# Half of the q and k transposes by the DMA crossbar, a reordered opening, sixteen matmuls moved to an earlier stage, and states scaled as soon as they are made

## The chip, the cores and the metric

The kernel runs on one core of one Trainium2 chip. The metric is device microseconds (us) per execution. Each timed kernel is run several times, in the same rounds as the kernel before on the same chip; I quote medians. "PE" is TensorE, "ACT" ScalarE, "DVE" VectorE, "POOL" GpSimd, "SP" SyncE.

## The reference, cut to what matters

Decayed linear attention (4 batches, 8 heads, 768 positions, head size 64), followed by a two-layer MLP (512 to 2048 to 512) with an ELU between the layers.

```python
# attention, per block; S is a state per head that decays and is carried along
intra = (q k^T * Dmask) v
inter = (q * lam^(pos+1)) S
out   = intra + inter
S     = lam^block * S + (k * rev_pow)^T v
# MLP on x = [3072, 512]
h = x @ w_in ;  g = where(h > 0, h, exp(min(h, 0)) - 1) ;  y = g @ w_out
```

## The kernel before

The kernel works in chunks of 128 positions of one batch: 24 chunks, numbered so that four in a row (one of each batch) make one MLP tile of 512 tokens. There are six tiles. While the MLP of a tile runs, the attention of the next tile is slipped in between its steps, two chunks per "visit". A visit has three places in the step list: transposes of q and k, then scores and mask, then output and state.

```python
def att_T(g, n, which, tag="S"):           # PE transposes q or k into PSUM
    ...
    nc.tensor.transpose(pt[:, j, i, hp, :], in_=nat[:, 2*hp : 2*hp+2, :], identity=ident16[:])
def att_Te(g, n, which, eng):              # ACT evicts them to SBUF, as qT and kT
    ...
    nc.scalar.copy(out=dst[:], in_=pt[:, j])

def att_tmp(g, eng="p"):                   # POOL: tmp = old state * lam^128
    ...
    e.tensor_tensor(out=tmp[r], in0=old[r, :, :, r], in1=up_p[r]..., op=ALU.mult)
def att_st(g):                             # DVE: new state = tmp + U (U is in PSUM)
    ...
    nc.vector.tensor_tensor(out=new[r, :, :, r], in0=tmps[g][r], in1=pu[r], op=ALU.add)

def mm1(t, n):  # 4 matmuls into psH, then ACT: e = exp(psH), r = relu(psH)
def elu(...):   # DVE: g = min(e - 1, r)
def mm2(t, i, n):  # one matmul of chunk i into psM; after n = 15 the eviction and the store

def visit(g, s0, s1, s2):
    at(s0, att_T / att_Te for q and k); at(s0, att_kd, g, 2)      # kd = k * ks, on DVE
    at(s1, att_S, g); at(s1, att_S, g+1); at(s1, att_mask, ...)   # P = psS * mask, on DVE
    at(s2, att_tmp, g)                                            # scaling, just ahead of its use
    at(s2, att_O, g, 2); at(s2, att_U, g); at(s2, att_X, g, 2); at(s2, att_st, g)

# steps: (name, mm1 of that step, [mm2 of that step])
('A', n): mm1 of tile 0, n = 0..15; from n = 10 mm2 of its chunks 0 and 1
('B', n): no mm1: mm2 of chunks 0 and 1 of tile 0 (B6 to B15), and attention of tile 1
(1, n):   mm1 of tile 1, and two mm2 of chunks 2 and 3 of tile 0
(2, n) to (5, n): mm1 of the tile, four mm2 of the tile before
```

In the opening, q, k and v of chunk 0 come as float32 over the hardware queues (SP, ACT) and are cast on DVE and ACT. All else comes over POOL's queue, which casts to fp16 on the way.

## Time and profile before

The kernel takes 229.4 us. Milestones, read from the starts of the exps (ACT, `e<-psH`; there are 16 per tile) in the trace:

| | first exp | 16th exp (end of A) | 17th (tile 1) | 33rd (tile 2) | 81st (tile 5) | span |
|---|---|---|---|---|---|---|
| before | 21.8 | 43.9 | 55.5 | 83.7 | 183.1 | 227.5 |

The window view gives the busy time of each engine between such milestones: after each window its length, then busy time (instructions) by engine, granted clock, DMA share, and GB/s.

```profile
core 0: us, PE busy (x) PEld busy (x) DVE busy (x) ACT busy (x) POOL busy (x), PEclk, DMA share, GB/s
0.00:21.80 21.80, 11.75 (x110) 6.41 (x111) 11.98 (x24) 9.60 (x21) 19.55 (x28) 1.00 1.69 152
21.80:43.90 22.10, 19.67 (x139) 8.85 (x138) 16.11 (x24) 16.58 (x31) 16.94 (x16) 0.92 1.79 180
43.90:83.70 39.80, 37.62 (x423) 21.07 (x422) 33.68 (x41) 24.59 (x42) 29.34 (x27) 1.00 2.46 167
83.70:183.10 99.40, 99.40 (x824) 50.85 (x822) 72.41 (x86) 65.28 (x114) 9.40 (x7) 1.00 0.34 43
```

In the fourth window PE is busy for the whole 99.40 us. In the three before it, several engines share the chain. A busy PE in this view is not a full PE, because matmuls overlap. So I also use a stricter count. PE's work is what its matmuls need back to back, as the trace shows them when nothing holds them (four of 512 columns in 0.86 us, sixteen transposes of 128 columns in 0.89 us, half of that for the paired ones on half the array); what is left between the starts of matmuls is idle.

| stretch of the kernel before | length | PE work | PE idle |
|---|---|---|---|
| 16th to 17th exp (the B steps) | 11.6 | 9.3 | 2.3 |
| 17th to 33rd exp (tile 1) | 28.2 | 26.2 | 2.0 |
| 33rd exp to 209 us (tiles 2 to 5) | 125.3 | 122.6 | 2.7 |

The page of the kernel before, in 40 slices (tenths): PE, the granted clock, and the DMA engines.

```profile
PE   0488969989998999999999999999999999999993
...
PEclk9999988999999999999999999999999999999999
DMA  4999999999999999210110110110110011001212
```

The granted clock is 0.5 for one stretch of 3.4 us, from 32.9 us, in the first pass. The DMA engines are full until about 90 us; nearly all of that is loading.

One line of waits (who waited for whom: us in total, times, longest):

```profile
DVE st L346 <- POOL tmp L328: 1.8, 3, 1.1
```

### The profile page before, as it was taken

To read this page: it belongs to the slowest core of one execution; us is meant where nothing else is said; L and a number is where in the kernel's file an instruction comes from. 1 tells how busy PE (TensorE), PEld (TensorE's weight loads), DVE (VectorE), ACT (ScalarE), POOL (GpSimd) and SP (SyncE) were. 2 spreads that over 40 slices of the span, in tenths; PEclk is the share of its full clock that TensorE was granted. 3 is DMA by queue.
4 is the path that set the end of the run, shared out by engine and by line. 5 is a ranking of instruction groups with operands and counts; after the bars stand their busy time and mean duration, and the time that the engine had idled before them with its cause. 6 is when DMAs were issued, how large, how long until landed. Compare 5 with 4: busy or idle time off the path is not lost.

```text
span 227.5 us, 4119 instructions
## 1 busy us (share of the span) xinstructions
PE 209.0 (92%) x1673; PEld 105.4 (46%) x1673; DVE 148.3 (65%) x193; ACT 135.9 (60%) x244; POOL 75.2 (33%) x75
## 2 busy tenths in 40 slices
PE   0488969989998999999999999999999999999993
PEld 0353425546454554554554554555455444444441
DVE  2549885798876999997887667647537544534110
ACT  4562686733859587576576576576486466676110
POOL 8899947838677893130220000000000000000000
PEclk9999988999999999999999999999999999999999
DMA  4999999999999999210110110110110011001212
GB/s 97 171 163 186 189 162 173 196 163 156 197 157 153 174 156 158 68 46 3 46 48 3 46 49 0 46 49 1 46 49 31 15 49 46 37 20 39 92 50 89
DMA packets 83971, 20.59 MB, mean 91 GB/s; under 512 B 76144, under 2 KB 81008, under 8 KB 83952
## 3 DMA queue, kind: packets, MB, share of 16 engines
q0 software_dynamic: 77088, 13.24, 84.3%
q1 hardware_dynamic: 5680, 6.69, 8.8%
q10 hardware_dynamic: 1184, 0.39, 0.7%
q8 instruction: 13, 0.21, 0.4%
q14 instruction: 6, 0.05, 0.1%
HBM read 27.27 MB, written 6.29 MB: 148 GB/s over the span
## 4 chain that ended last, share of the span: by engine, by line
PE 73%; DVE 10%; ACT 9%; issue 3%; DMA 2%; POOL 1%; SPq 0%; DVEq 0%; ACTq 0%
PE psM L387 33%; PE psH L359 29%; DVE P L256 5%; PE psT L210 4%; ACT e L364 3%; DMA q_first<-in_q_dram 2%; DVE g L379 2%; PE psO L269 2%; PE psS L244 2%; ACT r L368 2%; DVE xt L293 2%; PE psO L277 1%; ACT qT L221 1%; ACT kT L221 1%; POOL tmp L328 1%
## 5 line engine op out<-in xcount | busy, mean ns | idle before, releaser
L359 PE MATMUL psH<-xt,wi 128*128 128x512 f16 x384 | 98.8, 382 | 2.4 <-ACT r L368 2.3
L379 DVE SCALAR_TENSOR_TENSOR g<-e,r 128x512 f16<-128x512 f32 x92 | 68.6, 758 | 46.0 <-ACT r L368 45.4
L387 PE MATMUL psM<-wo,g 128*128 128x512 f16 x384 | 98.1, 381 | 0.0
L364 ACT ACTIVATE e<-psH 128x512 f32<-128x512 f32 x96 | 58.0, 605 | 57.9 <-PE psH L359 55.6
L359 PEld LDWEIGHTS <-wi 128*128 128x128 f16 x384 | 37.6, 98 | 48.7 <-issue 4.9
L368 ACT ACTIVATE r<-psH 128x512 f16<-128x512 f32 x92 | 55.4, 602 | 0.0
L387 PEld LDWEIGHTS <-g 128*128 128x128 f16 x384 | 35.6, 98 | 40.1 <-issue 0.6
L256 DVE TENSOR_TENSOR P<-psS,mask 128x1024 f16<-128x1024 f32 (+1 forms) x28 | 28.7, 1065 | 4.1 <-PE psS L244 3.8
L328 POOL TENSOR_TENSOR tmp<-st,up_p 64x512 f32<-64x512 f16 x16 | 20.2, 1261 | 22.6 <-DVE st L346 21.6
L293 DVE TENSOR_TENSOR xt<-psO,qs 128x1024 f16<-128x1024 f32 (+2 forms) x15 | 14.9, 1004 | 6.3 <-PE psO L277 5.4
L221 ACT COPY qT<-psT 128x1024 f16<-128x1024 f16 (+1 forms) x14 | 12.6, 896 | 7.1 <-PE psT L210 7.1
L78 POOL DMA_DIRECT2D kn<-in_k_dram x13 | 14.3, 1103 | 5.3 <-issue 4.7
L78 POOL DMA_DIRECT2D vn<-in_v_dram x13 | 14.5, 1114 | 4.5 <-issue 2.9
L78 POOL DMA_DIRECT2D qn<-in_q_dram x13 | 14.7, 1132 | 3.7 <-issue 1.8
L407 ACT COPY osb<-psM 128x512 f32<-128x512 f32 x12 | 7.1, 592 | 14.6 <-PE psM L387 14.6
L210 PE MATMUL psT<-ident,qn 128*128 128x128 f16 x96 | 8.4, 231 | 7.7 <-DVE qn L162 7.3
L269 PE MATMUL psO<-P,vn 128*64 128x128 f16 x192 | 12.6, 227 | 1.3 <-DVE P L256 0.8
L269 PEld LDWEIGHTS <-vn 128*64 128x64 f16 x192 | 10.1, 111 | 7.1 <-issue 6.2
L221 ACT COPY kT<-psT 128x1024 f16<-128x1024 f16 (+1 forms) x14 | 12.8, 916 | 0.0
L231 DVE TENSOR_TENSOR kd<-kn,ks 128x1024 f16<-128x1024 f16 x10 | 12.3, 1229 | 0.0
L210 PEld LDWEIGHTS <-qn 128*128 128x128 f16 x96 | 6.9, 103 | 11.7 <-DVE qn L162 7.3
L346 DVE TENSOR_TENSOR st<-tmp,psU 64x512 f16<-64x512 f32 x16 | 10.9, 681 | 2.0 <-POOL tmp L328 1.8
(43 smaller groups left out, 97.8 us busy)
## 6 DMA issues: line engine op xcount, KB each, us to landing
out_dram<-osb SPq DMA_DIRECT2D x23, 256.0 KB, 2.0
qn<-in_q_dram POOLq DMA_DIRECT2D x10, 256.0 KB, 12.9
kn<-in_k_dram POOLq DMA_DIRECT2D x10, 256.0 KB, 13.0
vn<-in_v_dram POOLq DMA_DIRECT2D x10, 256.0 KB, 13.2
wo<-in_moe_w_out_dram POOLq DMA_DIRECT2D x4, 512.0 KB, 14.0
wi<-in_moe_w_in_dram POOLq DMA_DIRECT2D x2, 512.0 KB, 6.8
wi<-in_moe_w_in_dram POOLq DMA_DIRECT2D x3, 256.0 KB, 6.8
qn<-in_q_dram POOLq DMA_DIRECT2D x3, 128.0 KB, 7.6
```

Of the source, the lines that this page charges most:

```text
L78: nc.gpsimd.dma_start(out=dst, in_=src[b : b + n, :, rows].rearrange("b h p d -> p (b h) d"))
L210: nc.tensor.transpose(pt[:, j, i, hp, :], in_=nat[:, 2 * hp : 2 * hp + 2, :], identity=ident16[:],)
L221: nc.scalar.copy(out=dst[:], in_=pt[:, j])
L256: nc.vector.tensor_tensor(out=P[:, :, c], in0=s[:, :, c], in1=mask[:, :, c], op=ALU.mult)
L269: nc.tensor.matmul(po[r, i, hp, :], lhsT=v_of(g + i, 2 * hp + hh), rhs=P[:, hh, hp, :], start=True, stop=(c == 0), skip_group_check=True,)
L293: nc.vector.tensor_tensor(out=xt[t][:, c, i * L : (i + n) * L].rearrange("p h (n l) -> p n h l", n=n), in0=po[:, :, c], in1=qs[:, c].unsqu ...
L328: e.tensor_tensor(out=tmp[r], in0=old[r, :, :, r], in1=up_p[r].unsqueeze(1).unsqueeze(3).broadcast_to([64, 2, HP, 64]), op=ALU.mult,)
L359: nc.tensor.matmul(pH[:], lhsT=wi[:, kk, j * 128 : (j + 1) * 128], rhs=xt[t][:, kk, :], start=(kk == 0), stop=(kk == HP - 1),)
L364: nc.scalar.activation(e[:], pH[:], AF.Exp)
L368: nc.scalar.activation(r[:], pH[:], AF.Relu)
L379: nc.vector.scalar_tensor_tensor(out=gt[t][:, n, :], in0=e[:], scalar=-1.0, in1=r[:], op0=ALU.add, op1=ALU.min)
L387: nc.tensor.matmul(pm[:], lhsT=gt[t][:, n, i * L : (i + 1) * L], rhs=wo_t[wo_at[n][0]][:, wo_at[n][1], :], start=(n == 0), stop=(n == NF - 1),
```

## The change

Its intent has three parts.

1. **Crossbar.** q and k of chunks 12 to 23 are transposed by DMA, from the loaded SBUF tiles to SBUF, instead of by PE with an eviction on ACT. The Trainium skill, "DMA: Bandwidth & Descriptors", section "DMA Transpose (X-bar)", says that the plain DMA transpose can be issued by the hardware queues only and that it takes 2-byte types; the kernel keeps to both (SP, fp16).
2. **Opening.** Chunk 0 comes over POOL's casting queue, first in line. Transposes of q and k are separate, with filler matmuls (`warm`) between. The states are cleared by DVE; `kd` of the first four chunks goes to POOL, and their state copies to ACT and to later steps (A8, A10). The first three hidden blocks of tile 0 are computed early, on the 384 columns that are there before chunk 3 (the "prefill").
3. **Middle.** The 16 `mm2` of chunk 2 of tile 0 move from tile 1 into the B steps (the "fill"). A state is scaled right after it is made ("early scaling"), not just ahead of its use.

Smaller edits came along: from tile 1 on the third place of a visit lies one step later, the visit in B lies one step earlier, hidden block 1 of tile 0 takes the ordinary path of exp and relu, and `tmp` has three buffers where it had two.

```diff
-    LOADS = [(1, 1, 'q'), (1, 1, 'k'), (1, 1, 'v'), (2, 1, 'q'), ...
+    LOADS = [(0, 1, 'q'), (0, 1, 'k'), (0, 1, 'v'), (1, 1, 'q'), ..., ('kd', 0), ('wi', 6), ('kd', 2), ...
+    def att_xT(g):
+        for j, ts in enumerate((qn, kn)):
+            dst = asb.tile([128, 2 * HP, 128], FP16, tag=f"{w}T", ...)
+            nc.sync.dma_start_transpose(out=dst[:], in_=heads(ts, g, 2).rearrange("p h d -> p (h d)"))
+    XT = {12: (1, 10), 14: (2, 2), 16: (2, 10), 18: (3, 2), 20: (3, 10), 22: (4, 2)}
     def visit(g, s0, s1, s2):
+        if g in XT:
+            at(XT[g], att_xT, g)
+        else: (transposes on PE as before)
-        at(s2, att_tmp, g)
         at(s2, att_O, g, 2)
         ...
         at(s2, att_st, g)
+        at(s2, att_tmp, g + B)
... (cut: opening, order of transposes, scores and warm-ups; prefill with mm1_mm(0, n, 0, 3 * L); places of the visits) ...
-(('B', 0), None, []), ...            ((1, 0), (1, 0), [(0, 2, 0), (0, 2, 1)]), ...
+(('B', 0), None, [(0, 2, 0)]), ...   ((1, 0), (1, 0), [(0, 3, 0)]), ...
```

## The prediction

> **What bounds the kernel now.** The stage view (busy time by windows) and the chain of waits show three regimes.
>
> 1. Opening, 0 to 20.8 us. The first full matmul of the MLP starts at 20.79 us. The chain begins with the load of q of chunk 0 (issued 1.17, landed 6.77 us) and then crawls through casts, ScalarE copies and VectorE masks. The loads of chunks 1 to 3, issued by POOL from 1.36 us, land 7.6 us after issue; they advance by about 0.87 us per 128 KB.
> 2. 20.8 to about 83 us: PE alternates with ScalarE and VectorE. In tile 0's first pass ScalarE needs 1.2 us per step (exp 605 ns, relu 602 ns) for 0.86 us of matmul; the granted clock even falls to 0.5 at 34 to 36 us. From about 45 to 54 us (the steps without new hidden activations) I count 6.8 us of PE work in 9.2 us, and the next tile, 54.3 to 83.2 us, holds 25.6 us of PE work in 28.9 us.
> 3. 83 us to the end: PE is never idle in the window view; the chain is matmul after matmul (four in 0.86 us). ScalarE (65%) and VectorE (50 to 80%) have room there.
>
> **What the change does.**
> - Transposes of chunks 12 to 23 leave PE: six groups of 16, each 0.89 us in the chain, all in regime 3. That is 5.3 us, all on the critical path. Twelve ScalarE evictions (1.03 us each) go too, off the path. In their place come twelve 256 KB crossbar DMAs on the SP queue, issued 8 steps (about 14 us) before use. The Trainium skill, "Advanced Engine Details and Errata", section X-Bar Transpose (TRN2), says they run as fast as ordinary DMAs. No trace here shows one yet. At the 12 to 16 us that loads need under the present traffic even the first would be just in time; later ones meet an idle DMA. I expect no PE wait from them.
> - Opening: chunk 0 goes first on the casting queue without the three 256 KB loads beside it and without two DVE casts (0.43 and 0.79 us) and one ScalarE cast. I estimate q of chunk 0 at about 5 us, v of chunk 3 at 15 to 16 us (16.0 now), and the first exp near 18 to 18.5 us instead of 21.85: gain about 3.5 us. Three hidden blocks are computed on three quarters of the columns beforehand. After that ScalarE still binds (about 21.8 us for the first pass, against 20 now), so little more comes there.
> - Refill: 16 output matmuls (3.5 us) move from the next tile into the steps without hidden activations, filling the holes there; that tile then is bound by ScalarE and VectorE at about 24 to 25 us. Early state scaling removes POOL waits (1.8 us before the state adds; 2.1 us of POOL scaling lies in the chain near 65 us). Together about 2 us.
>
> Sum: 5.3 + 3.5 + 2 = 10.8 us.
>
> **Prediction:** 218.8 us, range 214.5 to 224. Faster by over 2%: 0.91; within 2%: 0.08; slower by over 2%: 0.01.
>
> **What would show it.** PE transposes 192 down to 96; each half stage from 83 us on 16.7 down to about 15.8 us; first exp near 18 us; the stretch from the first step without hidden activations to the second tile's end 2 us shorter; SP transposes landing within 10 us; no PE wait on a transposed tile.
>
> **What would make it wrong.** Crossbar transposes far slower than ordinary loads, or slowing the POOL loads, so that scores wait for qT or kT; the first POOL load still landing 7 us after issue, which would hold the opening; ScalarE in the second tile costing more than the filling gains; output stores held up behind a waiting transpose on SP.

## More of the kernel before

POOL runs its instructions in order: DMA issues, `tmp`, and (before the change) the clearing of the states.

Groups of instructions of the kernel before that the change touches (busy, mean ns of one, idle before and its releaser):

```profile
L379 DVE SCALAR_TENSOR_TENSOR g<-e,r 128x512 f16<-128x512 f32 x92 | 68.6, 758 | 46.0 <-ACT r L368 45.4
...
L328 POOL TENSOR_TENSOR tmp<-st,up_p 64x512 f32<-64x512 f16 x16 | 20.2, 1261 | 22.6 <-DVE st L346 21.6
...
L231 DVE TENSOR_TENSOR kd<-kn,ks 128x1024 f16<-128x1024 f16 x10 | 12.3, 1229 | 0.0
...
L210 PE MATMUL psT<-ident,qn 128*128 128x128 f16 x96 | 8.4, 231 | 7.7 <-DVE qn L162 7.3 <-DVE xt L293 0.3
L210 PE MATMUL psT<-ident,kn 128*128 128x128 f16 x96 | 8.4, 230 | 0.1
```

## The result, and the profile after

The changed kernel takes 220.41 us (220.04 to 222.15, four runs), the kernel before 229.43. The ratio is 0.9617, with a 95% interval of 0.9558 to 0.9675. A ratio here is the mean time of one kernel's runs over that of the other's of the same rounds, so it is not quite the ratio of the medians. Timed a second time (experiment 9), it was 220.21 us, ratio 0.9605.

| | first exp | 16th | 17th | 33rd | 81st | span |
|---|---|---|---|---|---|---|
| before | 21.8 | 43.9 | 55.5 | 83.7 | 183.1 | 227.5 |
| after | 20.1 | 39.7 | 54.6 | 79.4 | 173.8 | 218.6 |
| gained so far | 1.7 | 4.2 | 0.9 | 4.3 | 9.3 | 8.9 |

The last row reads the result: 4.2 us are gained by the end of the first pass (A), 3.3 of them are lost again in the B steps, and come back in tile 1. From the 33rd to the 81st exp 5.0 us are gained, evenly.

The window view of the changed kernel:

```profile
0.00:20.10 20.10, 15.02 (x130) 7.51 (x131) 12.25 (x25) 9.54 (x21) 19.09 (x26) 1.00 1.63 127
20.10:39.70 19.60, 17.00 (x133) 7.98 (x131) 16.61 (x18) 17.72 (x33) 18.18 (x17) 1.00 1.80 183
39.70:79.40 39.70, 37.87 (x412) 20.69 (x413) 36.59 (x42) 24.67 (x42) 29.77 (x26) 1.00 2.19 172
79.40:173.80 94.40, 94.40 (x737) 45.92 (x736) 70.82 (x87) 55.00 (x103) 12.14 (x10) 1.00 0.79 84
```

The third window, B and tile 1 together, is as long as before (39.70 against 39.80 us), and DVE is now busy for 36.59 us of it instead of 33.68. In the fourth window PE is still always busy, with 87 fewer matmul records and 5.0 us less.

The slices of the changed kernel: in this profile the clock does not dip. (One of its four timed runs, the one of 222.15 us, has a mean clock of 0.992; more on this before the experiments.)

```profile
PE   5979789899998999999999999999999999999992
...
PEclk9999999999999999999999999999999999999999
DMA  6999999999999999999143052061011011110221
```

DMA issues of the changed kernel (count, size, median us from issue to landing); the two lines of the transposes.

```profile
qT<-qn SPq DMA_TRANSPOSE x6, 5.2
kT<-kn SPq DMA_TRANSPOSE x6, 5.2
```

The median hides two groups: six transposes that ran beside the loads landed 6.6 to 11.9 us after issue, the six later ones after 3.2 to 3.8 us. No line of the waits names a DMA of qT or kT.

The groups and the wait that answer to those shown before:

```profile
L398 DVE SCALAR_TENSOR_TENSOR g<-e,r 128x512 f16<-128x512 f32 x93 | 71.3, 780 | 37.5 <-ACT r L387 37.3
...
L336 POOL TENSOR_TENSOR tmp<-st,up_p 64x512 f32<-64x512 f16 x16 | 21.6, 1347 | 21.2 <-DVE st L355 20.3
...
L239 DVE TENSOR_TENSOR kd<-kn,ks 128x1024 f16<-128x1024 f16 x8 | 11.5, 1443 | 0.0
...
L206 PE MATMUL psT<-ident,kn 128*128 128x128 f16 x32 | 2.5, 219 | 0.7 <-DMA kn<-in_k_dram 0.7
L206 PE MATMUL psT<-ident,qn 128*128 128x128 f16 x32 | 2.4, 219 | 0.0
```

With 32 more of the opening, in tiles of their own (`psTq`, `psTk`), 96 transposes are left on PE.

The wait of the state add on POOL's scaling is gone from the list, but `kd` has become slower (1443 ns against 1229) and so has `g` (780 against 758). The timeline shows why. Each line has start, duration, engine, instruction, count. First the kernel before, where the scaling runs from 38.34 to 40.97 us, mostly in a pause of DVE of 2.12 us:

```profile
36.35 0.69 DVE L379 SCALAR_TENSOR_TENSOR g<-e,r 128x512 f16<-128x512 f32 x1 [1.37 <-ACT r L368]
...
36.96 1.22 DVE L231 TENSOR_TENSOR kd<-kn,ks 128x1024 f16<-128x1024 f16 x1
...
38.28 0.69 DVE L379 SCALAR_TENSOR_TENSOR g<-e,r 128x512 f16<-128x512 f32 x1
38.34 2.63 POOL L328 TENSOR_TENSOR tmp<-st,up_p 64x512 f32<-64x512 f16 x2
...
41.09 0.69 DVE L379 SCALAR_TENSOR_TENSOR g<-e,r 128x512 f16<-128x512 f32 x1 [2.12 <-ACT r L368]
```

Then the changed kernel, where four scalings run from 32.30 to 38.24 us:

```profile
29.35 0.68 DVE L398 SCALAR_TENSOR_TENSOR g<-e,r 128x512 f16<-128x512 f32 x1
...
31.97 1.94 DVE L398 SCALAR_TENSOR_TENSOR g<-e,r 128x512 f16<-128x512 f32 x1 [0.29 <-ACT r L387]
...
32.30 5.94 POOL L336 TENSOR_TENSOR tmp<-st,up_p 64x512 f32<-64x512 f16 x4
...
33.84 2.06 DVE L239 TENSOR_TENSOR kd<-kn,ks 128x1024 f16<-128x1024 f16 x1
...
35.82 2.97 DVE L398 SCALAR_TENSOR_TENSOR g<-e,r 128x512 f16<-128x512 f32 x2
...
38.71 2.34 DVE L264 TENSOR_TENSOR P<-psS,mask 128x1024 f16<-128x1024 f32 x2
```

A `g` needs 0.68 us alone and 1.94 us here; a `kd` 1.22 alone and 2.06 here. The Trainium skill, "SBUF — State Buffer", section "Who interferes with whom", says that a DVE instruction with two SBUF inputs contends with a GpSimd instruction that reads SBUF, and that the second of the two blocks until the first is done. The trace agrees: `g` (e and r) and `kd` (kn and ks) have two SBUF inputs and are slowed; `st`, whose second input is in PSUM, took 692 ns beside the scaling and 677 alone. Over the whole changed kernel 13 of 93 `g` ran beside the scaling, at 1344 ns against 689 for the others. Up to the 33rd exp this costs DVE about 7.3 us more than the same instructions alone; in the kernel before it is 2.5 us.

### The profile page after: what moved, and what is told of

Same layout as the page of the kernel before. It is cut to its first block, busy times and chain, and to the rows that moved or that the text cites. A ratio compares the mean times of both kernels' runs of the same rounds, so it can differ in the third digit from the quotient of the medians.

```text
span 218.6 us, 3968 instructions
## 1 busy us (share of the span) xinstructions
PE 204.8 (94%) x1593; PEld 100.3 (46%) x1593; DVE 150.3 (69%) x190; ACT 126.8 (58%) x234; POOL 79.2 (36%) x76
## 4 chain that ended last, share of the span: by engine, by line
PE 71%; DVE 13%; POOL 5%; ACT 5%; issue 2%; DMA 2%; DVEq 0%; POOLq 0%; ACTq 0%
PE psM L406 34%; PE psH L372 30%; DVE g L398 5%; DVE P L264 3%; PE psO L277 2%; DMA vn<-in_v_dram 2%; ACT e L383 2%; ACT r L387 2%; DVE kd L239 2%; POOL qn L72 2%; POOL kn L72 2%; PE psO L285 2%; PE psS L252 2%; POOL vn L72 1%; DVE st L355 1%
## 5 line engine op out<-in xcount | busy, mean ns | idle before, releaser
L372 PE MATMUL psH<-xt,wi 128*128 128x512 f16 (+2 forms) x396 | 98.0, 372 | 2.8 <-DVE g L396 1.1
L398 DVE SCALAR_TENSOR_TENSOR g<-e,r 128x512 f16<-128x512 f32 x93 | 71.3, 780 | 37.5 <-ACT r L387 37.3
L336 POOL TENSOR_TENSOR tmp<-st,up_p 64x512 f32<-64x512 f16 x16 | 21.6, 1347 | 21.2 <-DVE st L355 20.3
L72 POOL DMA_DIRECT2D vn<-in_v_dram x14 | 15.4, 1102 | 4.2 <-issue 4.2
L426 ACT COPY osb<-psM 128x512 f32<-128x512 f32 x12 | 7.0, 591 | 16.1 <-PE psM L406 16.1
L72 POOL DMA_DIRECT2D qn<-in_q_dram x14 | 15.7, 1124 | 1.4 <-issue 1.4
L72 POOL DMA_DIRECT2D kn<-in_k_dram x14 | 15.3, 1091 | 1.9 <-issue 1.9
L424 DVE COPY osb<-psM 128x512 f32<-128x512 f32 x11 | 7.6, 689 | 5.9 <-PE psM L406 5.8
L239 DVE TENSOR_TENSOR kd<-kn,ks 128x1024 f16<-128x1024 f16 x8 | 11.5, 1443 | 0.0
L355 DVE TENSOR_TENSOR st<-tmp,psU 64x512 f16<-64x512 f32 x16 | 10.9, 680 | 0.2
L285 PE MATMUL psO<-qT,st 128*64 128x128 f16 x160 | 10.3, 219 | 0.0
L285 PEld LDWEIGHTS <-st 128*64 128x64 f16 x160 | 9.0, 110 | 0.0
L252 PE MATMUL psS<-qT,kT 64*128 64x128 f16 x192 | 8.0, 221 | 0.9 <-ACT kT L218 0.8
```

Of the source, the lines that this page charges most:

```text
L72: nc.gpsimd.dma_start(out=dst, in_=src[b : b + n, :, rows].rearrange("b h p d -> p (b h) d"))
L239: e.tensor_tensor(out=kd[:].rearrange("p (n h) d -> p n h d", n=n), in0=heads(kn, g, n).rearrange("p (n h) d -> p n h d", n=n), in1=ks_b, ...
L285: nc.tensor.matmul(po[r, i, hp, :], lhsT=st[(g + i) % B // 2][c % 2][:, (g + i) % 2, hp, r], rhs=qT[g + i][:, hp, :], start=False, stop=Tr ...
L372: nc.tensor.matmul(pH[:, lo:hi], lhsT=wi[:, kk, j * 128 : (j + 1) * 128], rhs=xt[t][:, kk, lo:hi], start=(kk == 0), stop=(kk == HP - 1),)
L398: nc.vector.scalar_tensor_tensor(out=gt[t][:, n, :], in0=e[:], scalar=-1.0, in1=r[:], op0=ALU.add, op1=ALU.min)
```

## The experiments

Twelve kernels ran; all gave correct results. Totals are medians, ratios are to the kernel before in the same rounds.

| | what | total us | ratio | 16th to 33rd exp |
|---|---|---|---|---|
| before | | 229.4 | 1 | 39.8 |
| after | the change (experiment 9: again) | 220.41 (220.21) | 0.9617 (0.9605) | 39.7 (39.4) |
| 1 | change, all transposes on PE | 226.23 | 0.9856 | 40.0 |
| 2 | before, plus crossbar | 224.48 | 0.9783 | 40.0 |
| 3 | change, late scaling | 224.69 | 0.9794 | 43.3 |
| 4 | change, no fill | 221.60 | 0.9661 | 39.5 |
| 5 | change, late scaling and no fill | 222.01 | 0.9675 | 40.7 |
| 6 | change, fused state update on DVE | 220.58 | 0.9608 | 39.3 |
| 7 | change, crossbar from chunk 8 | 222.84 | 0.9716 | 41.0 |
| 8 | change, no prefill | 220.79 | 0.9624 | 39.5 |
| 10 | fused update, crossbar from chunk 10 | 218.44 | 0.9534 | 38.1 |
| 11 | change, chunk 0 over the hardware queues | 219.72 | 0.9584 | 39.2 |
| 12 | change, crossbar from chunk 10 | 218.53 | 0.9526 | 36.9 |

A caution for the small differences: among the kernels whose program is the same up to the 16th exp (after, 1, 4, 9, 12) that exp came between 39.7 and 40.6 us in the profiles. A single profile therefore doesn't settle differences under 1 us in the total. The experiments ran in three sessions on three chips (1 to 4, 5 to 8, 9 to 12); the kernel before took 229.32, 229.30 and 229.18 us there, so totals are compared across sessions.

A second caution is the granted clock. Four profiles (before, 3, 7, 8) show, in mid-kernel, one stretch of 3.4 us at a clock of 0.5: from 32.9, 72.7, 62.1 and 18.8 us. In experiment 3 the four matmuls of a hidden block took 1.71 us there, against 0.86. Each stretch began between 0.3 us before and 2.3 us after the end of a pause of PE of 1.6 to 3.2 us; but experiment 2 has a pause of 1.7 us in the same place as the kernel before, and no such stretch, so what sets it off stays open. One stretch lowers the mean clock of a run by 0.0075 (3.4 x 0.5 / 227.5; the profiled run of the kernel before has 0.992). I therefore read a mean of 0.993 or less as a run that had one. For the kernel before it makes no difference that can be seen: nine of its 31 timings beside the experiments are such runs, 229.4 us on average, against 229.3 for the others. But all 14 runs of experiments 3, 7 and 8 are such runs, and only one of the eight of the changed kernel, so their differences contain it.

### 1 and 2: the crossbar by itself

```diff
-    XT = {12: (1, 10), 14: (2, 2), ...}     # experiment 1, in the changed kernel
+    XT = {}
+    def att_xT(g): ...                       # experiment 2, in the kernel before, with XT and
+        if g in XT: at(XT[g], att_xT, g)     # the branch in visit, and nothing else
```

> The changed kernel with all transposes back on PE; everything else of the change stays. Theory (the crossbar saves PE issue time in a stage where PE never idles): slower than the changed kernel by six times 0.89 us, so about 225.7 us, a ratio to the kernel before of about 0.984; each half stage after the second tile goes from 15.7 back to 16.6 us. Rival (the transposes were covered or the crossbar costs something elsewhere): within 2 us of 220.4.

> The kernel before with the crossbar transposes of chunks 12 to 23 alone. Theory: 5.1 us faster than the kernel before, about 224.3 us, ratio 0.978, with the first 83 us unchanged to within 0.5 us. Rival (the crossbar works only with the rest, because it delays the loads or the stores in the older schedule): under 3 us faster.

Taking the crossbar away costs 5.8 us (226.23 against 220.41); adding it alone gains 4.8 us (224.48 against 229.32). From the 33rd to the 81st exp: before 99.4 us, experiment 1 99.4, experiment 2 94.5, after 94.4. The step of the prediction holds, and the crossbar needs nothing of the rest.

### 3: late scaling

```diff
+        at(s2, att_tmp, g)
         at(s2, att_O, g, 2)
...
-        at(s2, att_tmp, g + B)
```

> The changed kernel with the state scaled where it was before (just ahead of its use) and no other difference. My theory: the early scaling puts POOL beside VectorE operations that read two SBUF operands (g and kd), which cost 0.65 and 0.45 us more each there; on the chain that is about 2.3 us between the first tile's last exp and the next tile's first. So the late place should make that stretch 1 to 2.3 us shorter, give back up to 1.8 us of waits of the state add, and end between 218.5 and 220.5 us. Rival (early scaling helps as intended): 1 to 2 us slower, 221.4 to 222.4 us.

My theory fell. The kernel became 4.3 us slower, not faster (223.5 to 226.3 us, the slower runs at the lower clocks, 0.992 to 0.974). The part that I had foreseen is there: the stretch from the 16th to the 17th exp went from 14.9 to 13.8 us, and between the 16th and the 33rd exp only one `g`, at its start, is slowed. But tile 1 went from 24.8 to 29.5 us. The waits of the whole run:

```profile
DVE st L355 <- POOL tmp L336: 7.1, 6, 2.8
...
ACT e L383 <- DVE g L398: 6.0, 4, 3.7
...
PE psH L372 <- ACT r L387: 3.4, 2, 2.7
```

This is a chain over four engines. DVE runs in order, so when the state add waits for POOL's scaling, the `g` behind it waits too; ACT runs out of `e` buffers; PE runs out of `psH`. POOL is late because it also runs in order: ahead of the scaling stand the issues of the next loads. Timeline of POOL alone in experiment 3 (the bracket is idle time before the instruction):

```profile
60.24 1.14 POOL L72 DMA_DIRECT2D qn<-in_q_dram  x1 [1.62 <-issue]
62.68 1.14 POOL L72 DMA_DIRECT2D kn<-in_k_dram  x1 [1.31 <-issue]
64.44 1.14 POOL L72 DMA_DIRECT2D vn<-in_v_dram  x1 [0.62 <-issue]
65.65 2.14 POOL L336 TENSOR_TENSOR tmp<-st,up_p 64x512 f32<-64x512 f16 x2
```

POOL pauses between issues while the DMA engines are full. That it waits for room in the DMA queue is my reading; the profile calls it only "issue". So early scaling has two effects that I had taken for one: it slows DVE by sharing SBUF with it, and it takes POOL's slow queue out of DVE's path. The second is the larger.

Not all of the 4.7 us in tile 1 is this wait. The page of experiment 3 shows a pause of PE (the 3), and then a dip of the clock:

```profile
PE   5878879999993999999999999999999999999992
...
PEclk9999999999999699999999999999999999999999
```

In the timeline PE stands still for 2.7 us (67.8 to 70.5, waiting for ACT's relu, the chain above), and from 72.7 to 76.1 us the clock is 0.5, which costs some 1.7 us by the four matmuls timed there (an estimate). All six runs have a mean clock that says they had such a stretch, so no run shows what the wait costs without it.

### 4 and 5: the fill, with and without early scaling

```diff
-(('B', 0), None, [(0, 2, 0)]), ...   ((1, 0), (1, 0), [(0, 3, 0)]), ...
+(('B', 0), None, []), ...            ((1, 0), (1, 0), [(0, 2, 0), (0, 2, 1)]), ...
# experiment 5: this, and the edit of experiment 3
```

> The changed kernel with the output matmuls of the third chunk back in the second tile, as before. The stretch without hidden activations was 11.6 us before and 14.9 us after, the second tile 28.2 and 24.8 us. Theory A (the move only shifts PE work from one stretch to the other, because both are chains of VectorE, ScalarE and PE): within 0.7 us of the changed kernel, with the first stretch about 3 us shorter and the tile 3 us longer. Theory B (the fill works, and what hides its gain is the slower VectorE): 2 us or more slower than the changed kernel.

> Both parts of the middle undone: late scaling and no fill; opening and crossbar of the change stay. Completes a two by two table of the stretch from the last exp of tile 0 to the first of tile 2: early and fill 39.7 us, late and fill 43.3, early and no fill 39.5. If the two parts depend on each other (the fill makes tile 1 short enough for the POOL queue to hold up the state add, early scaling takes that away), this is about 39.8 us as in the kernel before, total about 221 us. If early scaling is worth its 3.6 us whatever the fill, it is about 43 us, total about 224.5.

Totals as a two by two table:

| | fill | no fill |
|---|---|---|
| early scaling | 220.41 (220.21) | 221.60 |
| late scaling | 224.69 | 222.01 |

The two depend on each other. Fill alone costs 2.7 us; early scaling alone gains 0.4 us; both together gain 1.6 to 1.8 us. With the fill, tile 1 has less PE work, so its visits come closer together and POOL's queue cannot keep up; early scaling takes that wait away.

What the fill does when scaling is early is seen from PE's idle time, counted as above, from the 16th to the 17th exp and from there to the 33rd:

| | B: length, PE idle | tile 1: length, PE idle | idle in both |
|---|---|---|---|
| before | 11.6, 2.3 | 28.2, 2.0 | 4.3 |
| no fill (4) | 12.9, 3.6 | 26.6, 0.9 | 4.5 |
| after | 14.9, 1.7 | 24.8, 2.5 | 4.2 |

The fill does close holes of B (3.6 to 1.7 us). But tile 1, which gave up the matmuls, opens new ones (0.9 to 2.5 us), which fits its steps of 5 matmuls (1.08 us) against two activations (1.2 us). The sum falls by 0.3 us, or by 1.1 us with the second profile of the change (experiment 9), which has 3.4 us. In the timing the fill is worth 1.2 us (221.60 against 220.41); the profiles show 0.9 us of that in the first pass, where both kernels have the same program. So the fill, with early scaling, is worth between 0.3 and 1.2 us; which, stays open.

### 6: no scaling on POOL at all

```diff
-                nc.vector.tensor_tensor(out=new[r, :, :, r], in0=tmps[g][r], in1=pu[r], op=ALU.add)
+                for hp in range(HP):
+                    nc.vector.scalar_tensor_tensor(
+                        out=new[r, :, hp, r], in0=old[r, :, hp, r], scalar=up_p[r, hp : hp + 1],
+                        in1=pu[r, :, hp], op0=ALU.mult, op1=ALU.add)
# and every call of att_tmp taken out
```

> The changed kernel with the state scaled and added in one VectorE instruction per head pair (eight small ones per pair of chunks that read one SBUF and one PSUM operand, in place of two adds and two POOL scalings). Theory (VectorE binds tile 1, and its g and kd lose 7.3 us beside POOL scaling before 80 us): no g over 0.8 us beside POOL any more, 1.5 to 2.5 us for the added instructions, the stretch from the last exp of tile 0 to the first of tile 2 shrinks from 39.7 to 36 to 38 us, total 216.5 to 219 us. Rival (the stretch is bound by PE and ScalarE, VectorE only follows): within 0.7 us of 220.4 or slower.

Groups of DVE in experiment 6:

```profile
L402 DVE SCALAR_TENSOR_TENSOR g<-e,r 128x512 f16<-128x512 f32 x93 | 62.8, 689 | 39.0 <-ACT r L391 38.8
...
L357 DVE SCALAR_TENSOR_TENSOR st<-st,up_p,psU 64x128 f16<-64x128 f16 x64 | 18.2, 344 | 0.1
```

All 93 `g` now average 689 ns: without scaling on POOL the slowing is gone, so the scaling is its cause. But the small instructions cost 344 ns each, 18.2 us in all against 10.9 for the adds. B became 1.4 us shorter (13.5), tile 1 1.0 us longer, and the total is the same as the changed kernel's (0.9608, interval 0.9581 to 0.9636). Up to the 33rd exp, DVE was spared the 7.3 us of contention and given some 3.7 us of dearer state updates (four of the eight pairs of chunks, 0.9 us each), so it had about 3.6 us less to do, and the total did not move by anything that the timing can tell: the rival holds. (Two of its six runs have a clock of 0.987 and 0.988; the other four average 220.0 us.)

### 7, 10 and 12: more chunks on the crossbar

```diff
-    XT = {12: (1, 10), ...}
+    XT = {8: ('B', 8), 10: (1, 2), 12: (1, 10), ...}   # 7, and the scores of 8 and 9 two steps later
+    XT = {10: (1, 2), 12: (1, 10), ...}                # 12; experiment 10 is this with experiment 6
```

> The changed kernel with chunks 8 to 11 transposed by the crossbar too, and the scores of 8 and 9 two steps later. PE loses 1.8 us and ScalarE 4.1 us of work in tile 1. If PE and ScalarE bind that tile, it shrinks by about 2 us, total about 218.4. If VectorE binds it (23.0 of 24.8 us busy), it moves by under 0.7 us. If the crossbar is late there (8 us beside the loads, loads of chunk 8 landing near 51 us), PE waits for kT and it gets slower.

> Fused state update of the run before, and chunks 10 and 11 on the crossbar too (their loads land near 57 us, their scores come near 70 us, so the 8 us of the crossbar beside loads should fit). It takes 0.9 us of PE, 2.0 us of ScalarE and the PE wait of 0.97 us for the k of chunk 10. If PE and its waits are the limit of tile 1: 1 to 1.9 us less than the fused kernel, 1.3 to 2.5 us less than the changed kernel. If VectorE binds: under 0.5 us less.

> Chunks 10 and 11 on the crossbar too, POOL scaling kept: the one part of the tenth experiment without the other. If the parts add up, 0.9 to 1.6 us less than the changed kernel; if transposes beside loads delay the later loads enough to reach the compute (in the seventh experiment q of chunks 12 and 13 landed at 71 us and not 62), no gain or slower.

From chunk 8 it is 2.4 us slower than the change. Waits of experiment 7 between 38 and 82 us:

```profile
PEld L252 <- DMA kT<-kn: 3.7, 1, 3.7
PE psS L252 <- DMA kT<-kn: 3.2, 1, 3.2
```

k of chunk 8 had landed at 52.4 us; its transpose was issued at 52.5 and landed at 62.3, 3.2 us too late for PE. At the end of this wait begins the stretch at a clock of 0.5 (62.1 us). In this profile 1.3 us of the loss lie before the 16th exp, where the program is that of the change, and 1.3 us after it. The transposes also share the DMA engines with the loads: q of chunk 12, which lands at 62.0 us in the changed kernel, landed at 71.0.

From chunk 10 the same step gains. Experiment 12 is at 218.53 us, 1.7 us less than the changed kernel in the same rounds (220.21; ratios 0.9526 and 0.9605, whose intervals of 0.9510 to 0.9541 and 0.9586 to 0.9624 don't touch). The transposes of chunk 10 took 9.6 and 11.3 us, and PE waited 0.3 us for them. PE's idle time from the 16th to the 33rd exp fell to 2.6 us (4.2 and 3.4 in the two profiles of the change), and its work by about 1 us. Among the holes that shrank is that of the changed kernel's worst wait there (between 54 and 80 us, PE and its weight loads waiting for ACT's copy of kT):

```profile
PEld L252 <- ACT kT L218: 1.7, 2, 1.3
...
PE psS L252 <- ACT kT L218: 0.8, 1, 0.8
```

The same wait in experiment 12:

```profile
PEld L252 <- ACT kT L218: 0.4, 1, 0.4
```

So tile 1 was held by PE and by ACT's evictions in front of the scores, not by DVE: 3.6 us less work for DVE brought nothing (6), and this step brought 1.7 us. (The slowing of `g` and `kd` up to the 33rd exp fell too in experiment 12, to 3.4 us; but between 6 and 10, which have none of it, the same step brought 2.1 us.) How much of it is PE's work and how much the wait for the evictions, no run separates. The fused update adds nothing to this (experiment 10: 218.44). Of the versions that beat both kernels clearly, 10 and 12, experiment 12 is the smaller edit.

### 8 and 11: the opening

```diff
-    for n in range(1): mm1_mm(0, n, 0, 3 * L, ...)         # 8: the early matmuls
-    for n in range(1, 3): mm1_mm(...);  for n in range(3): mm1_mm(0, n, 3 * L, 4 * L)
+    first = {...};  e.dma_start(out=first[w][:], in_=...)  # 11: chunk 0 as before, with its casts
-    LOADS = [(0, 1, 'q'), (0, 1, 'k'), (0, 1, 'v'), ...    #     (and two buffers of tmp, for room)
```

> The changed kernel without the early matmuls of the first three hidden blocks on three quarters of the columns. From the first to the fifth exp the kernel before took 5.9 us, the changed one 3.3. Theory A (the early matmuls bring that): the fifth exp comes about 2 us later, total about 222 us. Theory B (it is the reordering of the state work and ScalarE binds anyway): the fifth exp comes at most 0.7 us later, total within 0.7 us.

> The changed kernel with chunk 0 loaded as before: in float32 by the hardware queues, and cast on VectorE and ScalarE (and two buffers for the scaled state, for room). Theory of the prediction: first transposes near 7.3 us and not 5.0, first exp 1 to 2 us later, total 1 to 2 us more. Rival (the chip's DMA and the v of chunk 3 set the start of the MLP, v of chunk 3 landed at 16.1 us before and 17.6 after): first exp within 0.5 us, total within 0.6 us.

Without prefill the fifth exp comes 4.2 us after the first instead of 3.3 (before: 5.9), and the total is 220.79 us: the prefill brings 0.9 us there and 0.4 to 0.6 in the end, which the intervals (0.9602 to 0.9646, and 0.9558 to 0.9675 for the change) don't separate from nothing. The stretch at a clock of 0.5 lies just there in this profile (18.8 to 22.2 us), and all four runs have one; so the prefill may bring its 0.9 us by keeping the clock up, which no run tests.

Chunk 0 over the hardware queues makes the first transposes late, as expected. First the changed kernel, then experiment 11:

```profile
5.02 0.61 PE L206 MATMUL psTq<-ident,qn 128*128 128x128 f16 x4 [0.99 <-DMA qn<-in_q_dram]
```

```profile
7.20 0.61 PE L214 MATMUL psTq<-ident,qn 128*128 128x128 f16 x4 [3.18 <-DVE qn L162]
```

But the first exp came at 20.7 us (20.1 and 20.5 in the two profiles of the change), and the total was 219.72 us, 0.5 us less than the change in the same rounds. So the early landing of chunk 0 is worth nothing that these runs show. The chain of waits of the changed kernel says what is (start, duration, what):

```profile
12.60 4.99 DMA vn<-in_v_dram
17.63 0.30 PE psO L277 x4
```

The first full hidden block needs v of chunk 3, which lands at 17.6 us here, 16.1 in the kernel before and 17.1 in experiment 11. The loads come one after the other, whichever is first; and the changed list has two weight blocks (`wi` 0 and 1) ahead of v of chunk 3, which the kernel before has behind it (it was issued at 12.60 us, and at 9.24 before). The same shows later: k of chunk 4 landed at 33.1 us before and at 33.2 after, although the first pass runs some 4 us earlier, and PE's weight load waited 0.9 us for it.

## Why the prediction was right or wrong

The prediction was 218.8 us, range 214.5 to 224; measured were 220.4 and 220.2. Undoing the parts in turn gives a sum of totals: kernel before 229.4; with the crossbar 224.5 (minus 4.8); with the opening too, which is experiment 5, 222.0 (minus 2.5); with the middle too, which is the change, 220.3 (minus 1.7). The smaller edits count as opening here. In another order the parts differ by about 1 us: without the crossbar, opening and middle bring 3.1 us (experiment 1), and the crossbar then 5.8.

- **Crossbar, 5.3 us predicted, all on the critical path: right.** 4.8 us alone and 5.8 us as the last part; 5.0 us between the 33rd and 81st exp. The half stages fell from 16.6 to 15.7 us (predicted: 16.7 to 15.8), transposes on PE from 192 to 96, and PE never waited for a transposed tile. "Landing within 10 us" missed slightly: one k took 11.9 us.
- **Opening, 3.5 us predicted: the size was off, and so was the reason.** I tied it to chunk 0's landing and to v of chunk 3 at 15 to 16 us. Chunk 0 landed at 5.0 us, as estimated, and was worth nothing (experiment 11). v of chunk 3 came at 17.6 us, and the first exp at 20.1, not near 18. The opening brought 2.5 us in the total. In the profile most of it lies after the first exp, where I had expected little because ScalarE would hold the first pass at 21.8 us; it took 19.6 (22.1 before). From the first to the ninth exp the kernel before took 10.3 us, the changed one 7.6. There the kernel before had `kd` on DVE and the state copies on DVE and ACT. The prefill is 0.9 us of that, with the caution of experiment 8; what the rest is, no run separates. The clock is not it: the dip of the kernel before begins after its ninth exp (32.2 us), and its timings are the same with and without one.
- **Middle, 2 us predicted: the total fits, the mechanism was half right.** Both parts together gave 1.6 to 1.8 us, but filling holes is half of it at most: PE's idle time there is 4.2 and 3.4 us in the two profiles after, and 4.3 before. That 2 us came out near is therefore partly luck. I had counted 25.6 us of PE work in tile 1 where the stricter count finds 26.7 in the same window, and had not asked what tile 1 does when it gives matmuls away. What early scaling is for I had seen (waits of 1.8 us), but not how large these waits become once the fill is in (7.1 us in experiment 3).
- **Not foreseen:** the contention of POOL and DVE. It made DVE instructions 7.3 us longer up to the 33rd exp. Taking it away, at the price of dearer state updates, moved the total by nothing that the timing can tell (experiment 6).

## What to carry to other kernels

Work that is moved off an engine comes off the time one to one in a stage where that engine never idles (5.0 us measured for 5.3). Where it idles, anything can come of it: 3.5 us of matmuls moved into holes brought 0.3 to 1.2 us, because the holes moved too, and chunks 10 and 11 on the crossbar brought 1.7 us for about 1 us of PE work, because a wait went with it. So count the idle time of both places before and after. An in-order queue that issues loads is a bad place for work that another engine waits for: do such work as early as its inputs allow. Look at the clock of every profile before a difference is put down to a wait. A crossbar transpose is a DMA like others: let its data land well before, and give it the time that DMAs take at that point of the kernel, not in a quiet one.

## What the Trainium skill lacked or had wrong

- "Advanced Engine Details and Errata", section "X-Bar Transpose (TRN2)", says that transposes are as fast as regular DMAs. Here, with the DMA otherwise quiet, a transpose of 128 x 1024 fp16 (256 KB, SBUF to SBUF) landed 3.2 to 3.8 us after the start of its issue, while the median store of 256 KB (SBUF to DRAM) in the kernel before took 2.0 us. 1.3 us of the one and 0.33 of the other are the issue itself, so the transfers differ less (1.9 to 2.5 us against 1.7) than the totals.
- "DMA: Bandwidth & Descriptors", section "DMA Transpose (X-bar)", gives no figure for transposes beside POOL loads. Here they took 6.6 to 11.9 us, and in experiment 7 they delayed a load by 9 us (62.0 to 71.0).
- "SBUF — State Buffer", section "Who interferes with whom", was borne out (`g` 689 ns alone, 1344 beside POOL's scaling).
- No page that I used warns that work on POOL can stand behind its own load issues: 7.1 us of waits of DVE for POOL in experiment 3, and, with the dip of the clock that came along, 4.3 us in the total.
